# A decode attention kernel whose VectorE, ScalarE and sync-engine programs become loops with token waits

## The chip, the cores and the metric

The kernel runs on one core of a Trainium2 chip. The metric is the device time of one execution in microseconds (us), as the median of several runs. The profile is of one execution; its times count from the first instruction of the program.

## What is computed

One decode step of a transformer block, in float32, batch 1, one query token. Attention has 32 query heads in 8 groups; each group of 4 shares one key and value cache of 65536 rows by 128. The attention output and then a bilinear gated layer are added to the residual.

```python
B, Sq, D = x.shape                       # 1, 1, 512
Hq, Dh, Hkv = 32, 128, 8                 # cache: 8 x 65536 x 128, K and V
q = (layernorm(x) @ wq).reshape(...)     # 32 heads
scores = einsum("bhqd,bhkd->bhqk", q, k) * (Dh ** -0.5)
o = einsum("bhqk,bhkd->bhqd", softmax(scores), v)
h = x + o.reshape(B, Sq, Hq * Dh) @ wo
n = layernorm(h)
y = h + ((n @ w_gate) * (n @ w_up)) @ w_down   # 512 -> 1792 -> 512
```

## The kernel before

Each of the 8 cache heads is read in 4 K chunks and then 4 V chunks of 8.39 MB (128 partitions by 16384 values). Two SBUF buffers, `kv[0]` and `kv[1]`, take the chunks in turn, so a chunk can be fetched only when the one two before it has been used up. The sync engine (SP) issues all the large transfers, in one queue, in program order (lines 111 to 144): the first query weights `wq0`, the chunks, between V1 and V2 of each head one transfer `wqo` of 2.1 MB with the next head's query weights and this head's output weights, and at the end the gate, up and down weights `wg`, `wu`, `wd` into the two freed chunk buffers. The last V chunk, `wu` and `wd` are cut into pieces so that TensorE can begin on each piece as it lands.

TensorE (PE) already runs the heads as a hardware loop (line 388). A head there is: 16 small matmuls for the query (L333); for each K chunk 32 matmuls into a PSUM bank `psc` (L343); the softmax's transposes and small matmuls (L349 to L361); for each V chunk 32 matmuls into `pva` (L371); the sum over partitions (L378) and the output projection into `attn` (L384). Its waits are token waits: `take(s, n)` waits until semaphore `s` has `n` and subtracts them, so the same instruction serves every head.

The other engines have the 8 heads written out one after another, with waits on counters that only rise. ScalarE (ACT) copies each `psc` to SBUF (L210) and takes the exponentials (L235). VectorE (DVE) takes the maxima (L216), copies the transposes (L240), handles `orow`, `o_pad`, and adds the head's part to `acc` (L258). SP waits for a value of TensorE's counter, `pe.sem`, before each chunk (L116). After the loop the last head's sum goes to `arow` (L266), which also gives the sum for the second layer norm; the gate and up projections (L406), the product (L289) and the down projection (L437) follow, and the output is sent from L299.

The names in rows: `kv<-in_kT` and `kv<-in_v` are chunk transfers, `psc`, `ptp`, `pva`, `attn`, `sm` are PSUM banks. L315 is the `take` of TensorE.

Of the kernel before, what the change touches and what calls it, by code (L numbers as in the profile page):

```python
# [8 lines left out]
P = 128  # L9
# [13 lines left out]
PE_ONLY = bass.OrderedEngineSet([mybir.EngineType.PE])  # L23
# [20 lines left out]
def body(nc, xr, kT, v, wq0, wqo, wo7, wg, wu, wd, out):  # L44
# [33 lines left out]
    orow, acc, arow = tile("orow", P, 512), tile("acc", P, 512), tile("arow", P, 512)  # L78
# [14 lines left out]
    pe, dve, act, pool = (Counter(sem(n)) for n in ("pe", "dve", "act", "pool"))  # L93
    tok, atok = sem("tok"), sem("atok")
# [10 lines left out]
    def pe_at(h, m):  # L105
        return M_HEAD * h + m


# [3 lines left out]
    done = []  # L112
    for h in range(HKV):
        for i in range(2 * NT):
            if len(done) >= 2:
                sp.wait_ge(pe.sem, done[-2])  # L116
            buf = len(done) % 2
            if i == NT + 2:
                sp.wait_ge(pe.sem, pe_at(h, M_Q))
                if h < LAST:  # L120
                    sp.dma_start(wqo_sb, wqo[h]).then_inc(s_w, 16)
                else:
                    sp.dma_start(wo_sb, wo7).then_inc(s_w, 16)
            if h == LAST and i == 2 * NT - 1:
                for p, (lo, hi) in enumerate(zip(V_CUTS, V_CUTS[1:])):
                    cs = slice(lo * 512, hi * 512)
                    sp.dma_start(kv[buf][:, cs], v[h, i - NT][:, cs]).then_inc(s_vp[p], 16)
            else:
                src = kT[h, i] if i < NT else v[h, i - NT]
                whole = i == 2 * NT - 1  # L130
                sp.dma_start(kv[buf], src).then_inc(s_vp[0] if whole else s_kv[buf], 16)
                for p in s_vp[1:] if whole else ():

                    sp.sem_inc(p, 16)
            done.append(pe_at(h, M_K + i if i < NT else M_V + i - NT))
    sp.wait_ge(pe.sem, pe_at(LAST, M_V + 2))
# [4 lines left out]
    sp.wait_ge(pe.sem, pe_at(LAST, M_V + 3))  # L141
# [64 lines left out]
    for h in range(HKV):  # L206
# [5 lines left out]
        dve_e.wait_ge(pe.sem, pe_at(h, M_Q))  # L212
        dve_e.tensor_copy(q_pad[:, 28:28 + REP], sm[0][:, 0:REP]).then_inc(tok, 1)
        for s in range(NT):
            dve_e.wait_ge(act.sem, copies[s])
            i = dve_e.tensor_reduce(out=mx[:, s:s + 1], in_=sc[s], axis=AX.X, op=ALU.max)  # L216
            if s < 2:

                i.then_inc(tok, 1)
            else:  # L220
                dve.tick(i)
        dve_self()
        dve_e.tensor_reduce(out=m1, in_=mx, axis=AX.X, op=ALU.max).then_inc(tok, 1)
        dve_e.wait_ge(pe.sem, pe_at(h, M_MX))
        dve.tick(dve_e.tensor_reduce(
            out=mrow, in_=sm[1][0:1, 0:P].rearrange("p (g h) -> p h g", h=REP), axis=AX.X, op=ALU.max))
        dve_self()
        dve_e.tensor_copy(mexp, mrow.unsqueeze(1).to_broadcast([1, 32, REP])).then_inc(tok, 1)
        dve_e.wait_ge(pe.sem, pe_at(h, M_MB))
        c_bias = dve.tick(dve_e.tensor_scalar(  # L230
            out=nbias, in0=sm[0][:, 0:1], scalar1=-SCALE, scalar2=None, op0=ALU.mult))

        act_e.wait_ge(dve.sem, c_bias)
        for s in range(NT):
            act_e.activation(  # L235
                sc[s], sc[s], AF.Exp, bias=nbias[:, 0:1], scale=SCALE,
                accum_out=sums[:, s:s + 1]).then_inc(atok, 1)
        for s in range(NT):
            dve_e.wait_ge(pe.sem, pe_at(h, M_T + s))
# [21 lines left out]
    tail0 = pe_at(LAST, M_HEAD)
    (T_AC, T_G, T_PV, T_U, T_F0, T_F1, T_D) = range(tail0 + 1, tail0 + 8)

    dve_e.wait_ge(dve.sem, c_acc)
    dve_e.wait_ge(pe.sem, tail0)
    c_arow = dve.tick(dve_e.scalar_tensor_tensor(  # L266
        out=arow, in0=attn, scalar=1.0, in1=acc, op0=ALU.mult, op1=ALU.add, accum_out=rsum[:, 0:1]))
    dve_self()
    c_nmean = dve.tick(dve_e.tensor_scalar(
        out=nmean, in0=neg_mean, scalar1=rsum[:, 0:1], scalar2=None, op0=ALU.mult))  # L270
    dve_e.wait_ge(pe.sem, T_AC)
    c_hn = dve.tick(dve_e.tensor_copy(hn_pad[:, :, 0], sm[1][:, 0:KT]))
    dve_self()
    dve.tick(dve_e.tensor_tensor(out=ln_q2, in0=hn_pad[:, :, 0], in1=hn_pad[:, :, 0], op=ALU.mult))
    dve_self()
    c_s3 = dve.tick(dve_e.tensor_reduce(out=ln_s3, in_=ln_q2, axis=AX.X, op=ALU.add))
    act_e.wait_ge(pe.sem, T_PV)
    c_t3 = act.tick(act_e.activation(ln_t3, sm[0][:, 0:1], AF.Sqrt, bias=eps_t[:, 0:1], scale=1.0))
    dve_e.wait_ge(act.sem, c_t3)
    c_r3 = dve.tick(dve_e.reciprocal(ln_r3, ln_t3))  # L280

    act_e.wait_ge(dve.sem, c_r3)
    c_g = act.tick(act_e.activation(g_sb, psc[1][:, :FJ], AF.Copy, scale=ln_r3[:, 0:1]))
    dve_e.wait_ge(act.sem, c_g)
    dve_e.wait_ge(pe.sem, T_U)
    c_f = []
# [5 lines left out]
    dve_e.wait_ge(pe.sem, T_F0)
    c_fp0 = dve.tick(dve_e.tensor_copy(f_pad[:, 0:8, 0], sm[0][:, 0:8]))
    dve_e.wait_ge(pe.sem, T_F1)
    c_fp1 = dve.tick(dve_e.tensor_copy(f_pad[:, 8:NC, 0], sm[1][:, 0:6]))
    dve_e.wait_ge(pe.sem, T_D)
# [31 lines left out]
    take(s_wq, 16)  # L328

    def head():  # L330
# [4 lines left out]
        i.then_inc(pe.sem, 1)  # L335
        take(tok)
        for s in range(NT):
            take(s_kv[s % 2], 16)
            if s >= 2:
                take(tok)  # L340
# [6 lines left out]
            i.then_inc(pe.sem, 1)  # L347
        take(tok)
        pe_e.transpose(sm[1][0:1, 0:P], m1, ident).then_inc(pe.sem, 1)  # L349
        take(tok)  # L350
        mm(sm[0][:, 0:1], mexp.rearrange("p g h -> p (g h)"), ones[0:1, 0:1],  # L351
           start=True, stop=True).then_inc(pe.sem, 1)
        for s in range(NT):
            take(atok)
            if s >= 2:
                take(tok)
            for b in range(4):
                i = pe_e.transpose(ptp[s % 2][:, b * P:(b + 1) * P], sc[s][:, b * P:(b + 1) * P], ident)  # L358
            i.then_inc(pe.sem, 1)
        take(tok, 3)  # L360
        mm(sm[1][:, 0:REP], ones, l4, start=True, stop=True).then_inc(pe.sem, 1)  # L361
        for j in range(4):
            mm(pva[32 * j:32 * j + 32, :], zeros[:, 0:32], zeros, start=True, stop=False)  # L363
        for n in range(NT):
            vt = kv[n % 2]
            pieces = list(zip(V_CUTS, V_CUTS[1:])) if n == NT - 1 else [(0, 32)]
            for p, (lo, hi) in enumerate(pieces):
                take(s_vp[p] if len(pieces) > 1 else s_kv[n % 2], 16)
# [6 lines left out]
            i.then_inc(pe.sem, 1)  # L375
        take(tok)
# [9 lines left out]
        i.then_inc(pe.sem, 1)  # L386
# [4 lines left out]
    pe_e.wait_ge(dve.sem, c_arow)  # L391
    for k in range(KT):
        mm(sm[1][:, k:k + 1], arow[:, k * P:(k + 1) * P], sel_1, start=(k == 0), stop=False)
    pe_e.wait_ge(dve.sem, c_nmean)
    mm(sm[1][:, 0:KT], nmean, ones[:, 0:KT], start=False, stop=True).then_inc(pe.sem, 1)
    pe_e.wait_ge(dve.sem, c_hn)

    def project(acc, w, sems):
# [21 lines left out]
    i.then_inc(pe.sem, 1)  # L420
    pe_e.wait_ge(dve.sem, c_f[1])
# [17 lines left out]
    i.then_inc(pe.sem, 1)  # L439
# [41 lines left out]
```

## Time and profile before

| | us |
|---|---|
| median of 3 runs | 1309.79 (1309.71 to 1310.42) |
| span of the profiled execution, first to last instruction | 1308.5 |
| TensorE matmul busy | 712.9 (54% of the span) |
| VectorE busy | 73.5 (6%) |
| ScalarE busy | 47.2 (4%) |
| DMA queue of the large transfers, share of the 16 DMA engines | 99.7% |
| data read | 564.66 MB, 432 GB/s over the span |

The page gives busy time by engine, the span in 40 slices, the DMA queues and the chain of work that ended last. Behind it are views of single instructions in order of time, of waits, of one source line, and of stretches of the span. In these, "PEq" is TensorE's sequencer (its waits and branches), "SPq" the issuing of a transfer by SP. "Idle before" is the time in which the engine did nothing before a group, with what ended it. The granted TensorE clock averages 0.738 of full.

### The profile page before, as it was taken

The numbers are of one execution on the slowest core, as the hardware profiler recorded it, in microseconds if no ns is written. First come the engines' busy times: TensorE is split into PE (matmuls) and PEld (weight loads), VectorE is DVE, ScalarE is ACT, GpSimd is POOL, SyncE is SP. The second block draws the span as 40 slices with busy tenths as digits, with TensorE's granted clock in tenths as the row PEclk, the third lists the DMA queues.
The fourth block names the chain that finished last, engine by engine and source line by source line (L and its number), as shares of the span: only waits on it lengthen the run. The fifth ranks groups of instructions, "written<-read, shape, count | busy, mean of one in ns | idle before, by whom it ended". The sixth has DMA issues, their size and how long they took to land. (4 is left out here: it accounts for less than half of the span.)

```text
span 1308.5 us, 10559 instructions
## 1 busy us (share of the span) xinstructions
PE 712.9 (54%) x4938; PEld 249.0 (19%) x4938; DVE 73.5 (6%) x181; ACT 47.2 (4%) x102; POOL 2.5 (0%) x13
## 2 busy tenths in 40 slices
PE   5366384553755446563564636636365465655556
PEld 3012031210312112120131202212021121311113
DVE  0000000100001000010000100001000010000101
ACT  0000000100001000010000100001000010000100
POOL 0000000000000000000000000000000000000000
PEclk9777666776767867767767867678677677687778
DMA  9999999999999999999999999999999999999998
GB/s 417 427 435 445 421 445 425 441 425 441 425 441 425 441 429 441 441 429 437 429 439 427 441 425 441 427 441 437 435 435 431 439 417 450 425 441 425 441 420 374
DMA packets 12260, 564.80 MB, mean 432 GB/s; under 512 B 1365, under 2 KB 1369, under 8 KB 2010
## 3 DMA queue, kind: packets, MB, share of 16 engines
q1 hardware_dynamic: 12248, 564.67, 99.7%
q8 instruction: 6, 0.10, 0.0%
q14 instruction: 4, 0.03, 0.0%
q10 hardware_dynamic: 2, 0.00, 0.0%
HBM read 564.66 MB, written 0.00 MB: 432 GB/s over the span
## 5 line engine op out<-in xcount | busy, mean ns | idle before, releaser
L343 PE MATMUL psc<-kv,q_pad 128*32 128x512 f32 x2048 | 294.6, 740 | 256.2 <-PEq L315 256.2
L371 PE MATMUL pva<-kv,pt 128*16 128x512 f32 x2048 | 280.1, 707 | 276.9 <-PEq L315 276.8
L343 PEld LDWEIGHTS psc<-kv,q_pad 128*32 128x32 f32 x2048 | 81.3, 133 | 463.0 <-issue 463.0
L371 PEld LDWEIGHTS pva<-kv,pt 128*16 128x16 f32 x2048 | 67.1, 110 | 492.7 <-issue 492.7
L210 ACT COPY sc<-psc 128x512 f32<-128x512 f32 x32 | 18.7, 585 | 1144.3 <-PE psc L343 1144.3
L216 DVE TENSOR_REDUCE mx<-sc 128x1 f32<-128x512 f32 x32 | 21.9, 686 | 538.3 <-ACT sc L210 538.3
L333 PEld LDWEIGHTS sm<-xn,wqo_sb 128*128 128x128 f32 x256 | 49.1, 299 | 10.4 <-issue 10.4
L333 PE MATMUL sm<-xn,wqo_sb 128*128 128x1 f32 x256 | 49.8, 329 | 2.2 <-issue 2.2
L250 DVE COPY orow<-pva 128x512 f32<-128x512 f32 x8 | 5.5, 692 | 566.8 <-PE pva L371 566.8
L358 PE MATMUL ptp<-ident,sc 128*128 128x128 f32 x128 | 29.3, 396 | 10.2 <-PEq L315 9.7
L358 PEld LDWEIGHTS ptp<-ident,sc 128*128 128x128 f32 x128 | 21.4, 202 | 15.5 <-issue 14.7
L235 ACT ACTIVATE sc<-sc,nbias 128x512 f32<-128x512 f32 x32 | 22.7, 711 | 20.2 <-DVE nbias L230 20.2
L240 DVE COPY pt<-ptp 128x512 f32<-128x512 f32 x32 | 22.1, 691 | 21.6 <-PE ptp L358 21.6
L363 PE MATMUL pva<-zeros 128*32 128x512 f32 x64 | 12.9, 890 | 0.0
L384 PE MATMUL attn<-wqo_sb,o_pad 128*32 128x512 f32 x64 | 10.8, 749 | 3.4 <-PEq L315 3.4
L378 PE MATMUL sm<-sel_b,orow 128*128 128x4 f32 x64 | 8.2, 252 | 7.2 <-PEq L315 7.2
L378 PEld LDWEIGHTS sm<-sel_b,orow 128*128 128x128 f32 x64 | 7.7, 191 | 14.4 <-issue 14.4
L349 PE MATMUL sm<-ident,m 128*1 128x128 f32 x8 | 2.2, 269 | 13.6 <-PEq L315 13.6
L406 PE MATMUL psc<-kv,hn_pad 128*32 128x448 f32 x64 | 8.2, 651 | 1.9 <-DMA kv<-in_wu 1.0
L361 PE MATMUL sm<-l,ones 128*128 128x4 f32 x16 | 3.9, 312 | 9.6 <-PEq L315 9.6
L351 PE MATMUL sm<-ones,mexp 1*128 1x1 f32 x16 | 3.4, 279 | 5.7 <-PEq L315 5.7
L235 ACT ACTIVATION_READ_ACCUMULATOR sc<-sc,nbias 128x1 f32 x32 | 6.0, 187 | 0.0
(88 smaller groups left out, 68.6 us busy)
## 6 DMA issues: line engine op xcount, KB each, us to landing
wqo_sb<-in_wqo SPq DMA_DIRECT2D x7, 2048.0 KB, 15.2
kv<-in_v SPq DMA_DIRECT2D x1, 4096.0 KB, 21.7
kv<-in_wg SPq DMA_DIRECT2D x1, 3584.0 KB, 18.8
kv<-in_v SPq DMA_DIRECT2D x1, 2048.0 KB, 26.2
kv<-in_v SPq DMA_DIRECT2D x2, 1024.0 KB, 29.1
kv<-in_wu SPq DMA_DIRECT2D x1, 1792.0 KB, 23.0
kv<-in_wu SPq DMA_DIRECT2D x2, 896.0 KB, 25.5
kv<-in_wd SPq DMA_DIRECT2D x1, 1536.0 KB, 19.7
```

Of the source, the lines that this page charges most:

```text
L210: copies.append(act.tick(act_e.copy(sc[s], psc[s % 2])))
L216: i = dve_e.tensor_reduce(out=mx[:, s:s + 1], in_=sc[s], axis=AX.X, op=ALU.max)
L235: act_e.activation(sc[s], sc[s], AF.Exp, bias=nbias[:, 0:1], scale=SCALE, accum_out=sums[:, s:s + 1]).then_inc(atok, 1)
L240: dve_e.tensor_copy(pt[s].rearrange("p g b h -> p b g h"), ptp[s % 2].rearrange("p (b g h) -> p b g h", b=4, h=REP)).then_inc(tok, 1)
L333: i = mm(sm[0][:, r:r + 1], wq_sb[:, k, r * P:(r + 1) * P], xn[:, k:k + 1], start=(k == 0), stop=(k == KT - 1))
L343: i = mm(psc[s % 2][32 * j:32 * j + 32, :], q_pad[:, 28 - 4 * rs:60 - 4 * rs], kv[s % 2][:, (4 * rs + j) * 512:(4 * rs + j + 1) * 512], st ...
L358: i = pe_e.transpose(ptp[s % 2][:, b * P:(b + 1) * P], sc[s][:, b * P:(b + 1) * P], ident)
L363: mm(pva[32 * j:32 * j + 32, :], zeros[:, 0:32], zeros, start=True, stop=False)
L371: i = mm(pva[32 * j:32 * j + 16, :], pt[n][:, 8 * j + rs, :, :].rearrange("p b h -> p (b h)"), vt[:, w * 512:(w + 1) * 512], start=False, ...
L378: i = mm(sm[0][:, 0:REP], orow[:, b * P:(b + 1) * P], sel_b[:, 4 * b:4 * b + 4], start=(b == 0), stop=(b == 3))
L384: i = mm(attn[32 * r:32 * r + 32, :], o_pad[:, r, :], wo_sb[:, r, :], start=True, stop=True)
L406: i = mm(acc[32 * j:32 * j + 32, :FJ], hn_pad[:, k, :], w[:, o:o + FJ], start=(k == 0), stop=(k == KT - 1))
```

## The change

ScalarE, VectorE and SP get hardware loops over the heads. SP's loop has 7 rounds and the last head is written out behind it; the addresses of the chunks come from registers. TensorE's one rising counter is replaced by tokens: `pd` (TensorE to VectorE), `pa` (TensorE to ScalarE), `ad` and `da` (between ScalarE and VectorE), `own` (VectorE to itself), and `free`, one for each chunk buffer that may be filled. `free` is raised twice by SP at the start, by ScalarE for each K chunk, by TensorE for V0, V1 and V2, and by VectorE for V3. The three engines' programs begin with an alignment to a multiple of 128 instructions. The last head is no longer a special case on VectorE: every round runs the fused add with the row sum, into `acc`, and `arow` is gone.

```diff
+    def take(e, s, n=1):
+        e.wait_ge(s, n).then_inc(s, -n)
+
+    for e in (sp, act_e, dve_e):
+        e.addr_align(SLOTS, 0, max_nops=0)
...
+    sp.sem_inc(free, 2)
+
+    def chunks(h, last):
         for i in range(2 * NT):
-            if len(done) >= 2:
-                sp.wait_ge(pe.sem, done[-2])
-            buf = len(done) % 2
+            take(sp, free)
+            buf = i % 2
...
+    with nc.Fori(0, LAST, engines=SP_ONLY) as h:
+        chunks(h, False)
+    chunks(LAST, True)
...
-    for h in range(HKV):
-        copies = []
-        for s in range(NT):
-            act_e.wait_ge(pe.sem, pe_at(h, M_K + s))
-            copies.append(act.tick(act_e.copy(sc[s], psc[s % 2])))
+    with nc.Fori(0, HKV, engines=ACT_ONLY):
+        for s in range(NT):
+            take(act_e, pa)
+            act_e.sem_inc(free, 1)
+            act_e.copy(sc[s], psc[s % 2]).then_inc(ad, 1)
+        take(act_e, da)
...
+    with nc.Fori(0, HKV, engines=DVE_ONLY):
+        take(dve_e, pd)
...
-        dve_e.wait_ge(pe.sem, pe_at(h, M_V + NT - 1))
+        take(dve_e, pd)
+        dve_e.sem_inc(free, 1)
         dve_e.tensor_copy(orow, pva).then_inc(tok, 1)
...
-            c_acc = dve.tick(dve_e.tensor_tensor(out=acc, in0=attn, in1=acc, op=ALU.add))
+        take(dve_e, pd)
+        dve_e.scalar_tensor_tensor(
+            out=acc, in0=attn, scalar=1.0, in1=acc, op0=ALU.mult, op1=ALU.add,
+            accum_out=rsum[:, 0:1]).then_inc(own, 1)
+        take(dve_e, own)
...
-            i.then_inc(pe.sem, 1)
+            i.then_inc(pd if n == NT - 1 else free, 1)
```

On SP, one head before, from its third chunk on; `[waits pe]` is the wait on TensorE's counter, part of the transfer's own row:

```order
L131 DMA kv0<-in_kT 128x16384 [waits pe]
L131 DMA kv1<-in_kT 128x16384 [waits pe]
L131 DMA kv0<-in_v 128x16384 [waits pe]
L131 DMA kv1<-in_v 128x16384 [waits pe]
L121 DMA wqo_sb<-in_wqo 128x4096 [waits pe]
L131 DMA kv0<-in_v 128x16384
L131 DMA kv1<-in_v 128x16384 [waits pe]
```

The same engine in the changed kernel, from the start of its program; an ISA row at L128 or L125 is register arithmetic on an address, ahead of which the token is taken:

```order
L110 ISA [waits barrier_Pool_Activation_PE_DVE_SP_release]
L114 DMA wqo_sb<-in_wq0 128x2048
L138 UNCONDITIONAL_BRANCH
L128 ISA [waits free]
L128 DMA kv0<-in_kT 128x16384
L128 DMA kv0<-in_v 128x16384 [waits free]
L128 DMA kv1<-in_v 128x16384 [waits free]
L125 ISA [waits free]
L125 DMA wqo_sb<-in_wqo 128x4096
L134 DMA kv1<-in_v 128x16384 [waits free]
L138 REGISTER_ALU
L138 COMPARE_AND_BRANCH
```

The order of the transfers is the same; ahead of the first one stands the alignment (L110), and between it and the first chunk the loop's entry, a token and the address arithmetic.

On ScalarE before, the first head and the end of the program (ACT_TABLE_LOAD loads a function table; it stands once for the exponentials and once for the second square root, without a wait):

```order
L210 COPY sc<-psc 128x512 [waits pe] x4
L235 ACT_TABLE_LOAD
L235 ACTIVATE sc,sums<-sc,nbias 128x512 [waits dve]
L235 ACTIVATE sc,sums<-sc,nbias 128x512 x3
L278 ACT_TABLE_LOAD
L278 ACTIVATE ln_t<-sm,eps_t 128x1 [waits pe]
L283 ACTIVATE g_sb<-psc,ln_r 128x448 [waits dve]
```

On ScalarE in the changed kernel, the loop and what follows it:

```order
L215 ACT_TABLE_LOAD [waits pa]
L215 COPY sc<-psc 128x512
L215 COPY sc<-psc 128x512 [waits pa] x3
L218 ACTIVATE sc,sums<-sc,nbias 128x512 [waits da]
L218 ACTIVATE sc,sums<-sc,nbias 128x512 x3
L211 REGISTER_ALU
L211 COMPARE_AND_BRANCH
L277 ACT_TABLE_LOAD [waits pa]
L277 ACTIVATE ln_t<-sm,eps_t 128x1
L283 ACTIVATE g_sb<-psc,ln_r 128x448 [waits da]
```

The table load has moved into the loop, ahead of the copy of K0 and behind its token, and the load for the second square root now stands behind TensorE's token as well. In the loop's code the `sem_inc(free, 1)` stands between the token and the table load.

## Rows read from the trace of the kernel before

**Rows 1.** The page: the 40 slices, mean busy share of the DMA engines, in tenths.

```profile
DMA  9999999999999999999999999999999999999998
```

**Rows 2.** The page, DMA queues: packets, MB, share of 16 engines.

```profile
q1 hardware_dynamic: 12248, 564.67, 99.7%
q8 instruction: 6, 0.10, 0.0%
q14 instruction: 4, 0.03, 0.0%
```

**Rows 3.** Stretches of the span: us, busy by engine, granted clock, DMA share, GB/s.

```profile
core 0: us, PE busy (x) PEld busy (x) DVE busy (x) ACT busy (x) POOL busy (x), PEclk, DMA share, GB/s
0.00:2.00 2.00, 0.00 (x0) 0.00 (x0) 0.31 (x3) 0.72 (x1) 1.25 (x9) 1.00 0.29 34
2.00:100.00 98.00, 48.88 (x308) 21.53 (x309) 6.48 (x24) 6.45 (x12) 1.23 (x6) 0.81 1.01 437
...
1100.00:1200.00 100.00, 55.99 (x368) 19.99 (x368) 3.76 (x7) 1.75 (x3) 0.00 (x0) 0.72 1.00 433
...
1306.00:1308.50 2.50, 0.37 (x8) 0.10 (x8) 0.29 (x1) 0.00 (x0) 0.00 (x0) 1.00 0.00 1
```

**Rows 4.** Line L131, the chunk transfers from 30 us on.

```profile
L131 SPq DMA_DIRECT2D kv<-in_v x31: 327/328/447, 74.7 to 1227.1; - x31
L131 SPq DMA_DIRECT2D kv<-in_kT x30: 327/328/328, 34.1 to 1170.7; - x30
...
DMA to landing us min/median/max: 26.9/29.4/35.9
```

**Rows 5.** The chain that ended last, its end: start us, us, what.

```profile
1283.06 22.84 DMA kv<-in_wd
1305.90 0.04 issue
1305.94 0.47 PE pva L437 x8
1306.41 0.02 issue
1306.44 0.29 DVE y L297
```

**Rows 6.** In order of time, the start: start us, us, what [idle before].

```profile
0.73 0.52 ACTq L109 DMA_DIRECT2D x_row<-in_xr  x1
...
0.73 0.40 SPq L111 DMA_DIRECT2D wqo_sb<-in_wq  x1
...
1.20 0.88 SPq L131 DMA_DIRECT2D kv<-in_kT  x2
...
2.27 0.34 PE L320 MATMUL psc<-ones,x_row 1*128 1x1 f32 x1 [2.27 <-DMA x_row<-in_xr]
```

**Rows 7.** The page, DMA issues: KB each, us to landing.

```profile
wqo_sb<-in_wq SPq DMA_DIRECT2D x1, 1024.0 KB, 4.8
```

**Rows 8.** Line L388, the branches of TensorE's loop, ns.

```profile
L388 PEldq COMPARE_BRANCH  x8: 88/223/238, 179.0 to 1283.7; - x8
```

**Rows 9.** In order of time: a VectorE result taken by token, and a chunk's end.

```profile
103.69 0.23 DVE L245 TENSOR_SCALAR l<-sel_h,l 128x4 f32<-128x4 f32 x1
104.03 0.50 PEld L361 LDWEIGHTS sm<-l,ones 128*128 128x128 f32 x2 [1.57 <-issue]
...
197.47 0.33 SPq L131 DMA_DIRECT2D kv<-in_kT  x1
197.48 0.58 ACT L210 COPY sc<-psc 128x512 f32<-128x512 f32 x1 [96.55 <-PE psc L343]
```

**Rows 10.** VectorE's and ScalarE's waits: us in total, times, longest.

```profile
ACT sc L210 <- PE psc L343: 1144.3, 32, 96.5
...
DVE q_pad L213 <- PE sm L333: 43.9, 8, 7.1
```

**Rows 11.** Lines L235 and L278: table loads, ns and start.

```profile
L235 ACT ACT_TABLE_LOAD  x1: 1283/1283/1283, 95.2 to 95.2; - x1
L278 ACT ACT_TABLE_LOAD  x1: 1283/1283/1283, 1215.1 to 1215.1; - x1
```

**Rows 12.** In order of time, the end of the program.

```profile
1288.68 4.78 PE L406 MATMUL psc<-kv,hn_pad 128*32 128x448 f32 x32 [0.87 <-DMA kv<-in_wg]
...
1294.29 0.64 ACT L283 ACTIVATE g_sb<-psc,ln_r 128x448 f32<-128x448 f32 x1 [0.23 <-DVE ln_r L280]
...
1297.39 0.96 PE L406 MATMUL psc<-kv,hn_pad 128*32 128x448 f32 x8 [1.02 <-DMA kv<-in_wu]
1298.51 0.81 DVE L289 SCALAR_TENSOR_TENSOR f_sb<-psc,ln_r,g_sb 128x256 f32<-128x256 f32 x2 [4.25 <-PE psc L406]
...
1303.47 2.28 PE L437 MATMUL pva<-kv,f_pad 128*32 128x128 f32 x56 [0.84 <-DMA kv<-in_wd]
```

More of the change, by code (lines that the diff above doesn't have):

```diff
@@ L22 @@
 LAST = HKV - 1
-PE_ONLY = bass.OrderedEngineSet([mybir.EngineType.PE])
+PE_ONLY, DVE_ONLY, ACT_ONLY, SP_ONLY = (bass.OrderedEngineSet([e]) for e in (
+    mybir.EngineType.PE, mybir.EngineType.DVE, mybir.EngineType.Activation, mybir.EngineType.SP))
+SLOTS = 128
 V_CUTS = (0, 16, 24, 28, 32)
@@ L77, in body @@
     l4, linv = tile("l4", P, REP), tile("linv", P, REP)
-    orow, acc, arow = tile("orow", P, 512), tile("acc", P, 512), tile("arow", P, 512)
+    orow, acc = tile("orow", P, 512), tile("acc", P, 512)
     rsum, nmean = tile("rsum", P, 1), tile("nmean", P, P)
@@ L91, in sem @@
         return sems[-1]
-    pe, dve, act, pool = (Counter(sem(n)) for n in ("pe", "dve", "act", "pool"))
-    tok, atok = sem("tok"), sem("atok")
+    dve, act, pool = (Counter(sem(n)) for n in ("dve", "act", "pool"))
+    tok, atok, pd, pa, ad, da, own, free = (
+        sem(n) for n in ("tok", "atok", "pd", "pa", "ad", "da", "own", "free"))
     s_kv = [sem("s_kv0"), sem("s_kv1")]
@@ L103, in body @@
     wd_t = kv[1]
-    def pe_at(h, m):
-        return M_HEAD * h + m
+    def take(e, s, n=1):
+        e.wait_ge(s, n).then_inc(s, -n)
+    for e in (sp, act_e, dve_e):
+        e.addr_align(SLOTS, 0, max_nops=0)
     act_e.dma_start(x_row, xr).then_inc(s_xr, 16)
     sp.dma_start(wq_sb, wq0).then_inc(s_wq, 16)
-    done = []
-    for h in range(HKV):
+    sp.sem_inc(free, 2)
+    def chunks(h, last):
         for i in range(2 * NT):
-            if len(done) >= 2:
-                sp.wait_ge(pe.sem, done[-2])
-            buf = len(done) % 2
+            take(sp, free)
+            buf = i % 2
             if i == NT + 2:
-                sp.wait_ge(pe.sem, pe_at(h, M_Q))
-                if h < LAST:
+                if last:
+                    sp.dma_start(wo_sb, wo7).then_inc(s_w, 16)
+                else:
                     sp.dma_start(wqo_sb, wqo[h]).then_inc(s_w, 16)
-                else:
-                    sp.dma_start(wo_sb, wo7).then_inc(s_w, 16)
-            if h == LAST and i == 2 * NT - 1:
+            src = kT[h, i] if i < NT else v[h, i - NT]
+            if i < 2 * NT - 1:
+                sp.dma_start(kv[buf], src).then_inc(s_kv[buf], 16)
+            elif last:
                 for p, (lo, hi) in enumerate(zip(V_CUTS, V_CUTS[1:])):
                     cs = slice(lo * 512, hi * 512)
-                    sp.dma_start(kv[buf][:, cs], v[h, i - NT][:, cs]).then_inc(s_vp[p], 16)
+                    sp.dma_start(kv[buf][:, cs], src[:, cs]).then_inc(s_vp[p], 16)
             else:
[L129 to L132, printed above, removed]
+                sp.dma_start(kv[buf], src).then_inc(s_vp[0], 16)
+                for p in s_vp[1:]:
                     sp.sem_inc(p, 16)
-            done.append(pe_at(h, M_K + i if i < NT else M_V + i - NT))
-    sp.wait_ge(pe.sem, pe_at(LAST, M_V + 2))
+    with nc.Fori(0, LAST, engines=SP_ONLY) as h:
+        chunks(h, False)
+    chunks(LAST, True)
+    take(sp, free)
     sp.dma_start(wg_t, wg).then_inc(s_wg, 16)
@@ L140, in body @@
         sp.dma_start(wu_t[:, cs], wu[:, cs]).then_inc(s_wu[p], 16)
-    sp.wait_ge(pe.sem, pe_at(LAST, M_V + 3))
+    take(sp, free)
     for p, (lo, hi) in enumerate(zip(D_CUTS, D_CUTS[1:])):
@@ L237, in body @@
                 accum_out=sums[:, s:s + 1]).then_inc(atok, 1)
+    with nc.Fori(0, HKV, engines=DVE_ONLY):
+        take(dve_e, pd)
+        dve_e.tensor_copy(q_pad[:, 28:28 + REP], sm[0][:, 0:REP]).then_inc(tok, 1)
         for s in range(NT):
-            dve_e.wait_ge(pe.sem, pe_at(h, M_T + s))
+            take(dve_e, ad)
+            dve_e.tensor_reduce(out=mx[:, s:s + 1], in_=sc[s], axis=AX.X, op=ALU.max).then_inc(
+                tok if s < 2 else own, 1)
+        take(dve_e, own, 2)
+        dve_e.tensor_reduce(out=m1, in_=mx, axis=AX.X, op=ALU.max).then_inc(tok, 1)
+        take(dve_e, pd)
+        dve_e.tensor_reduce(
+            out=mrow, in_=sm[1][0:1, 0:P].rearrange("p (g h) -> p h g", h=REP), axis=AX.X,
+            op=ALU.max).then_inc(own, 1)
+        take(dve_e, own)
+        dve_e.tensor_copy(mexp, mrow.unsqueeze(1).to_broadcast([1, 32, REP])).then_inc(tok, 1)
+        take(dve_e, pd)
+        dve_e.tensor_scalar(
+            out=nbias, in0=sm[0][:, 0:1], scalar1=-SCALE, scalar2=None, op0=ALU.mult).then_inc(da, 1)
+        for s in range(NT):
+            take(dve_e, pd)
             dve_e.tensor_copy(
@@ L242, in body @@
                 ptp[s % 2].rearrange("p (b g h) -> p b g h", b=4, h=REP)).then_inc(tok, 1)
-        dve.tick(dve_e.tensor_reduce(out=l1, in_=sums, axis=AX.X, op=ALU.add))
-        dve_self()
+        dve_e.tensor_reduce(out=l1, in_=sums, axis=AX.X, op=ALU.add).then_inc(own, 1)
+        take(dve_e, own)
         dve_e.tensor_scalar(
             out=l4, in0=sel_h, scalar1=l1[:, 0:1], scalar2=None, op0=ALU.mult).then_inc(tok, 1)
-        dve_e.wait_ge(pe.sem, pe_at(h, M_L))
-        dve.tick(dve_e.reciprocal(linv, sm[1][:, 0:REP]))
@@ L249, in body @@
-        dve_e.wait_ge(pe.sem, pe_at(h, M_V + NT - 1))
+        take(dve_e, pd)
+        dve_e.reciprocal(linv, sm[1][:, 0:REP]).then_inc(own, 1)
+        take(dve_e, pd)
+        dve_e.sem_inc(free, 1)
         dve_e.tensor_copy(orow, pva).then_inc(tok, 1)
-        dve_self()
-        dve_e.wait_ge(pe.sem, pe_at(h, M_PO))
+        take(dve_e, own)
+        take(dve_e, pd)
         dve_e.tensor_tensor(
             out=o_pad[:, :, 0], in0=sm[0][:, 0:REP], in1=linv, op=ALU.mult).then_inc(tok, 1)
-        if h < LAST:
-            dve_e.wait_ge(dve.sem, c_acc)
-            dve_e.wait_ge(pe.sem, pe_at(h, M_AT))
-            c_acc = dve.tick(dve_e.tensor_tensor(out=acc, in0=attn, in1=acc, op=ALU.add))
@@ L261, in body @@
[L261 to L286, printed above, removed]
+        take(dve_e, pd)
+        dve_e.scalar_tensor_tensor(
+            out=acc, in0=attn, scalar=1.0, in1=acc, op0=ALU.mult, op1=ALU.add,
+            accum_out=rsum[:, 0:1]).then_inc(own, 1)
+        take(dve_e, own)
+    dve_e.sem_inc(tok, 1)
+    dve_e.tensor_scalar(
+        out=nmean, in0=neg_mean, scalar1=rsum[:, 0:1], scalar2=None, op0=ALU.mult).then_inc(tok, 1)
@@ new lines, in body @@
+    take(dve_e, pd)
+    dve_e.tensor_copy(hn_pad[:, :, 0], sm[1][:, 0:KT]).then_inc(own, 1)
+    take(dve_e, own)
+    dve_e.sem_inc(tok, 1)
+    dve_e.tensor_tensor(
+        out=ln_q2, in0=hn_pad[:, :, 0], in1=hn_pad[:, :, 0], op=ALU.mult).then_inc(own, 1)
+    take(dve_e, own)
+    dve_e.tensor_reduce(out=ln_s3, in_=ln_q2, axis=AX.X, op=ALU.add).then_inc(tok, 1)
+    take(act_e, pa)
+    act_e.activation(
+        ln_t3, sm[0][:, 0:1], AF.Sqrt, bias=eps_t[:, 0:1], scale=1.0).then_inc(ad, 1)
@@ L287, in body @@
+    take(dve_e, ad)
+    dve_e.reciprocal(ln_r3, ln_t3).then_inc(da, 1)
+    take(act_e, da)
+    act_e.activation(g_sb, psc[1][:, :FJ], AF.Copy, scale=ln_r3[:, 0:1]).then_inc(ad, 1)
+    take(dve_e, ad)
+    take(dve_e, pd)
     for half in range(2):
         cs = slice(half * 256, min(FJ, half * 256 + 256))
-        c_f.append(dve.tick(dve_e.scalar_tensor_tensor(
+        dve_e.scalar_tensor_tensor(
             out=f_sb[:, cs], in0=psc[0][:, cs], scalar=ln_r3[:, 0:1], in1=g_sb[:, cs],
-            op0=ALU.mult, op1=ALU.mult)))
@@ L292, in body @@
[L292 to L296, printed above, removed]
+            op0=ALU.mult, op1=ALU.mult).then_inc(tok, 1)
+    take(dve_e, pd)
+    dve_e.tensor_copy(f_pad[:, 0:8, 0], sm[0][:, 0:8]).then_inc(tok, 1)
+    take(dve_e, pd)
+    dve_e.tensor_copy(f_pad[:, 8:NC, 0], sm[1][:, 0:6]).then_inc(tok, 1)
+    take(dve_e, pd)
@@ L327, in body @@
     pe_e.wait_ge(dve.sem, c_const)
-    take(s_wq, 16)
+    take(pe_e, s_wq, 16)
     def head():
@@ L334, in head @@
                        start=(k == 0), stop=(k == KT - 1))
-        i.then_inc(pe.sem, 1)
-        take(tok)
+        i.then_inc(pd, 1)
+        take(pe_e, tok)
         for s in range(NT):
-            take(s_kv[s % 2], 16)
+            take(pe_e, s_kv[s % 2], 16)
             if s >= 2:
-                take(tok)
+                take(pe_e, tok)
             for rs in range(8):
@@ L367, in head @@
             for p, (lo, hi) in enumerate(pieces):
-                take(s_vp[p] if len(pieces) > 1 else s_kv[n % 2], 16)
+                take(pe_e, s_vp[p] if len(pieces) > 1 else s_kv[n % 2], 16)
                 for w in range(lo, hi):
@@ L374, in head @@
                            start=False, stop=(n == NT - 1 and rs == 7))
-            i.then_inc(pe.sem, 1)
-        take(tok)
+            i.then_inc(pd if n == NT - 1 else free, 1)
+        take(pe_e, tok)
         for b in range(4):
@@ L379, in head @@
                    start=(b == 0), stop=(b == 3))
-        i.then_inc(pe.sem, 1)
-        take(s_w, 16)
-        take(tok)
+        i.then_inc(pd, 1)
+        take(pe_e, s_w, 16)
+        take(pe_e, tok)
         for r in range(REP):
@@ L385, in head @@
                    start=True, stop=True)
-        i.then_inc(pe.sem, 1)
+        i.then_inc(pd, 1)
     with nc.Fori(0, HKV, engines=PE_ONLY, hint_back_edge=True):
         head()
-    pe_e.wait_ge(dve.sem, c_arow)
+    take(pe_e, tok)
     for k in range(KT):
[L393 to L396, printed above, removed]
+        mm(sm[1][:, k:k + 1], acc[:, k * P:(k + 1) * P], sel_1, start=(k == 0), stop=False)
+    take(pe_e, tok)
+    mm(sm[1][:, 0:KT], nmean, ones[:, 0:KT], start=False, stop=True).then_inc(pd, 1)
+    take(pe_e, tok)
     def project(acc, w, sems):
@@ L407, in project @@
                        start=(k == 0), stop=(k == KT - 1))
-        i.then_inc(pe.sem, 1)
+        return i
     project(psc[1], wg_t, [s_wg])
-    pe_e.wait_ge(dve.sem, c_s3)
-    mm(sm[0][:, 0:1], mean_m, ln_s3, start=True, stop=True).then_inc(pe.sem, 1)
+    take(pe_e, tok)
+    mm(sm[0][:, 0:1], mean_m, ln_s3, start=True, stop=True).then_inc(pa, 1)
     for j in range(4):
-        mm(pva[32 * j:32 * j + 32, 0:P], sel_pad, arow[:, j * P:(j + 1) * P], start=True, stop=False)
-    project(psc[0], wu_t, s_wu)
-    pe_e.wait_ge(dve.sem, c_f[0])
+        mm(pva[32 * j:32 * j + 32, 0:P], sel_pad, acc[:, j * P:(j + 1) * P], start=True, stop=False)
+    project(psc[0], wu_t, s_wu).then_inc(pd, 1)
+    take(pe_e, tok)
     for b in range(2):
@@ L419, in body @@
                start=(b == 0), stop=(b == 1))
-    i.then_inc(pe.sem, 1)
-    pe_e.wait_ge(dve.sem, c_f[1])
+    i.then_inc(pd, 1)
+    take(pe_e, tok)
     mm(sm[1][:, 0:4], f_sb[:, 2 * P:3 * P], sel_q, start=True, stop=False)
@@ L426, in body @@
                 start=False, stop=True)
-    i2.then_inc(pe.sem, 1)
+    i2.then_inc(pd, 1)
     fill(4)
-    pe_e.wait_ge(dve.sem, c_fp0)
+    take(pe_e, tok)
     for c in range(NC):
         if c == 8:
-            pe_e.wait_ge(dve.sem, c_fp1)
+            take(pe_e, tok)
         if c in D_CUTS:
```

45 lines of the change are left out of this document (11 added, 34 removed).

## Prediction

> **What bounds the kernel now.** I read the page first: in its slices the reader sees the DMA engines at nine tenths or more in 39 of 40 slices [rows 1], and in its queues one queue with 99.7% of the 16 engines' time [rows 2]. TensorE is at 54%, VectorE at 6%, ScalarE at 4%. An average could still hide gaps at the head boundaries, so the second view is the span cut into stretches [rows 3]: from 2 us on the DMA share is 1.00 (a share a little above 1 is packets counted where they start), at 433 to 437 GB/s, whatever TensorE and its clock do in the stretch; it falls to 0.00 only behind 1306 us. The stream of 564.67 MB therefore sets the time, and the kernel is three pieces: about 1.8 us before data flows (up to 2.00 us the share is 0.29), the stream up to the last landing at 1305.90, and 2.6 us of closing work to 1308.5.
>
> The third view says how much delay this stream can bear. SP issues a chunk when the one two before it is used up, and from then a chunk takes 26.9 us at least and 29.4 in the median until it lands, over 61 chunks [rows 4]. Alone, 8.39 MB at 433 GB/s take 19.4 us. So at each issue the queue still held 26.9 - 19.4 = 7.5 us of earlier work at the least, 10 us in the median. I call this the lead: a delay of the issue below 7.5 us moves no byte.
>
> The fourth view is the end of the chain [rows 5]: the last piece of `wd` lands at 1305.90, eight matmul records (0.47 us), VectorE's copy (0.29 us) and the output's transfer follow. Between them lie 0.04 and 0.02 us.
>
> **The change part by part.** The sum is made against the profiled execution, 1308.5 us of span; the median of the runs is 1309.79, which is 1.29 us more around the span. I leave these 1.29 us as they are.
>
> *SP's start.* Ahead of the first transfer, at 0.73 us [rows 6], stands the alignment. If the padding is jumped over, that is one branch. The only branches in the trace are those that close TensorE's loop: 88 ns the one that fell through, 223 to 238 ns those that were taken [rows 8], so 0.09 to 0.24 us where the code is already there; I take 0.15, near the middle, since the jump goes forward and compares nothing. Nothing hides this: all bytes come later by it. Between `wq` and the first chunk come a semaphore write, the loop's entry, a token and the arithmetic on the address. A token is priced by a row: VectorE's `l4` ends at 103.92 and TensorE, which takes a token for it, starts loading at 104.03 [rows 9], so 0.11 us, against 0.04 for a wait in the instruction itself [rows 5]; with a branch and two register steps like it this makes 0.5 to 0.8 us. `wq` lands 4.8 us after its issue [rows 7], at 5.5 us, and the chunk's issue moves from 1.20 to at most 2.0; from the issue of a small transfer to the matmul that uses it lie 2.27 - 0.73 = 1.54 us [rows 6], so its first bytes would be there by 3.6. Hidden, with 1.9 us in hand.
>
> *SP's chunk waits.* Each of the 64 chunks is now released by a token. For K chunks ScalarE stands between: TensorE, ScalarE's token, its `free`, SP's token. Before, SP and ScalarE reacted to the same end of a chunk within 0.01 us, at 197.47 and 197.48 [rows 9], so the added hop is two tokens, 0.22 us, and at the most 0.5 with the address arithmetic. ScalarE is never late for it: it waited 1144.3 us in total at these copies [rows 10], and `free` is raised before the copy and the table load. V3 goes over VectorE, which likewise waits there. Against a lead of 7.5 us: 0. With the lead gone it would cost 64 x 0.2 to 0.5 = 13 to 32 us, and that is what this term would be in a kernel with single chunks in flight.
>
> *Back edges.* SP's comes behind V3's issue, when its next token is more than ten microseconds away. ScalarE's comes after the exponentials, a whole V phase before its next token. VectorE's is the tight one: it comes behind the add to `acc`, and next is `q_pad`, for which VectorE waited 43.9 us in 8 heads, 5.5 each [rows 10]. With a branch of 0.24 and a token of 0.11 it keeps 5 us.
>
> *Table loads.* ScalarE's load of 1.28 us [rows 11] is now done in every head, ahead of the copy of K0. VectorE and TensorE get that copy 1.28 us later, and TensorE needs its `psc` bank again only for K2, two chunk landings of 19.4 us later: 0. At the end the load stood at 1215.1, out of the way; now it stands behind TensorE's token at about 1293.8, so `g_sb` moves from 1294.29 + 0.64 = 1294.93 to about 1296.3. The product that needs it began at 1298.51, behind `wu`'s last piece and the matmuls of 1297.39 [rows 12]. It has 2.2 us left: 0.
>
> *The last head's end.* VectorE's fused add is now followed by a token to itself, the loop's closing branch (88 ns when it falls through [rows 8]) and another semaphore write before TensorE goes on: 0.3 to 0.5 us. TensorE later waits 0.87 us for `wg`, 1.02 for `wu` and 0.84 for `wd` [rows 12], so each such delay is taken up by the next landing. Behind the product two PSUM copies with tokens add some 4 x 0.07 = 0.3 us, against the 0.84. Behind the last landing only VectorE's wait ahead of `y` becomes a token: 0.11 - 0.04 = 0.07 us, on the path.
>
> *Less code to load.* The instruction queues move 0.13 MB of 564.80 [rows 2]. At 432 GB/s the four packets of q14, 0.03 MB, are 0.07 us of the stream; they lie inside the span before and should go.
>
> Sum: 0.15 + 0.07 - 0.07 = +0.15 us. 1309.79 + 0.15 is 1309.9.
>
> **The rivals.** About 0.2%, 2.6 us, is what a measurement of this kernel can tell from no change.
>
> *A: the start waits for code (slower).* The alignment puts SP's first transfer into another block of code than the barrier ahead of it. If that block isn't there, SP stands still between the barrier and `wq`, and the whole stream with it, since there is no lead yet. The trace shows no such fetch, so the nearest rows bound it: a small transfer from issue to use, 1.54 us [rows 6], to the 4.8 us of `wq` under the first load [rows 7]. That gives 1311.4 to 1314.7; it is slower in my sense from a stall of 2.5 us on. Against it speaks that before, SP went from barrier to transfer without a pause the trace shows, and that ahead of the span there is time for loading. Taken at 3 us: 1312.9.
>
> *B: back edges that wait for code (slower, much).* The same fetch at each of VectorE's or SP's branches, in the full stream. VectorE has 5 us, then 7.5 us of lead: below 12.5 us nothing is seen, which a fetch of 1.5 to 4.8 us doesn't reach. If it had to wait like a chunk, 29.4 us, each of 7 heads would lose up to 17 us: 1309.8 + 119 = 1429. In its favour is only that the trace of before shows just TensorE's back edges, at 0.24 us. The Trainium skill speaks for this rival: "Runtime: NRT & Kernel Launch", section "Instruction fetch mechanics", says that a taken branch to code outside the blocks held must wait for a fetch, and so prefers unrolled code. In this trace TensorE's loop pays no such wait, and the loops of the change are far shorter than TensorE's; by that rule, too, they would stay inside what is held.
>
> *C: faster.* Only what lies outside the stream can shrink: 1.8 + 2.6 + 1.3 = 5.7 us. To gain 2.6 the shorter programs would have to halve it; I see no row for that. Nor would loops that did not save any fetch show: that is the forecast plus 0.07.
>
> **How the numbers follow.** Forecast 0.87: 1309.9, with 1309.0 to 1311.0 from the terms' own bounds (0.09 to 0.24 at the start, 0 to 0.2 at the end, and the runs' own spread of 0.7). A 0.09, half of it below the line of 1312.4 and half above. B 0.02. C 0.02. So faster 0.02, same 0.91, slower 0.07. The range takes the forecast's and the lower part of A: 1308.9 to 1311.8.
>
> **What would show it.** In the changed kernel's profile: the DMA share still 1.00 in every stretch; SP's first transfer within 0.3 us of the barrier (if it stands 1.5 us or more behind it, A); chunks that land 26 us or more after their issue, some 0.3 us less than before; eight table loads at the K0 copies and ScalarE still waiting there; q14 without packets in the span; the last `wd` landing 2.6 us before the end. Wrong would be a stretch with a share under 0.99 in mid-span, or a chain whose end is no longer `wd`.

## The result, and the profile after

The changed kernel takes 1312.37 us in the median of 18 runs (1311.99 to 1315.87), the kernel before 1309.86 in 18 runs (1309.71 to 1310.42); the ratio is 1.0021, 95% interval 1.0014 to 1.0028. It is 2.5 us slower. The forecast was 1309.9, at most 1311.8. The profiled execution spans 1311.4 us, against 1308.5; with 1312.75 us it is 0.4 us above the median of the runs.

The stream is as full as before. The page of the changed kernel, its DMA slices and queues (as [rows 1, 2]):

```profile
DMA  9999999999999999999999999999999999999998
...
q1 hardware_dynamic: 12248, 564.67, 99.5%
q8 instruction: 6, 0.10, 0.0%
q14 instruction: 3, 0.02, 0.0%
```

The stretches of the changed kernel (columns as in [rows 3]) show where it is not: in the first 4 us no data flow, only the three packets of q14 (12 GB/s up to 2 us).

```profile
0.00:2.00 2.00, 0.00 (x0) 0.00 (x0) 0.32 (x3) 0.00 (x0) 1.23 (x9) 1.00 0.04 12
2.00:4.00 2.00, 0.00 (x0) 0.00 (x0) 0.00 (x0) 0.22 (x1) 1.24 (x6) 1.00 0.00 0
4.00:100.00 96.00, 45.87 (x301) 19.63 (x301) 6.33 (x23) 4.95 (x7) 0.00 (x0) 0.83 1.01 436
```

In order of time, the start of the changed kernel (start us, us, what), to be read beside [rows 6]:

```profile
1.19 2.56 ACTq L112 DMA_DIRECT2D x_row<-in_xr  x1
1.23 2.33 SPq L114 DMA_DIRECT2D wqo_sb<-in_wq  x1
1.41 0.17 DVE L169 MEMSET ones<- 128x128 f32 x1 [1.41 <-PEq L469]
...
4.06 0.36 SPq L128 DMA_DIRECT2D kv<-in_kT  x1
```

SP's first transfer starts 0.5 us later, at 1.23 instead of 0.73, and its issue takes 2.33 us instead of 0.40. ScalarE's first transfer shows the same, 2.56 against 0.52. VectorE, aligned like them, only starts later (1.41 against 0.83) and then runs at once. SP's issue ends at 3.56 instead of 1.13: 2.43 us, which is the loss but for a rest. The packets of q14, of the kind "instruction", carry code, 0.01 MB each; I call them code packets. All three of the span are here; from 2.5 us to the end there is none. The DMA queues between 1.5 and 2.5 us:

```profile
q14 instruction: 3, 0.02, 8.5%
```

At the other end, the last landing and the copy behind it (as [rows 5]):

```profile
1308.73 0.43 PE L433 MATMUL pva<-kv,f_pad 128*32 128x128 f32 x8 [0.19 <-DMA kv<-in_wd]
1309.33 0.29 DVE L296 COPY y<-pva 128x128 f32<-128x128 f32 x1 [5.53 <-DVEq L107]
```

The last piece's matmuls come 2.79 us later than before (1305.94), the copy 2.89 (1306.44). So of 2.9 us in this execution 2.43 are lost at the start, 0.1 behind the last landing, and 0.36 are added inside the stream. The median loss of 2.5 us is as large as the first two together.

### The profile page after: what moved, and what is told of

It is laid out like the page before. It is cut to its first block, busy times and chain, and to the rows that moved or that the text cites. A ratio compares the mean times of both kernels' runs of the same rounds, so it can differ in the third digit from the quotient of the medians.

```text
span 1311.4 us, 11033 instructions
## 1 busy us (share of the span) xinstructions
PE 705.4 (54%) x4938; PEld 250.2 (19%) x4938; DVE 73.4 (6%) x188; ACT 56.1 (4%) x109; POOL 2.5 (0%) x13
## 5 line engine op out<-in xcount | busy, mean ns | idle before, releaser
L367 PE MATMUL pva<-kv,pt 128*16 128x512 f32 x2048 | 275.0, 697 | 276.4 <-PEq L107 276.4
L359 PE MATMUL pva<-zeros 128*32 128x512 f32 x64 | 8.5, 605 | 0.0
```

The source lines that it names most:

```text
L367: i = mm(pva[32 * j:32 * j + 16, :], pt[n][:, 8 * j + rs, :, :].rearrange("p b h -> p (b h)"), vt[:, w * 512:(w + 1) * 512], start=False, ...
```

## The experiments

**Theories.** *Alignment*: SP's first transfer is held because of the alignment. *Loops* (rival): loop entry, tokens and register addresses delay the transfers. *Any fetch* (rival): the code fetches, whichever engine they are for, delay the first data.

A *block* is here a stretch of 128 instructions, the unit of the alignment, and a *slot* a place in it; a block is *fresh* when the engine comes to it for the first time by a jump. A *fetch* shows as a code packet. The *hold* is the time by which the issue of a transfer is longer than its 0.40 us (SP) or 0.52 us (ScalarE) before.

### Which part of the change, and which engine

`e1_no_align`: the change without its alignments.

```diff
-    for e in (sp, act_e, dve_e):
-        e.addr_align(SLOTS, 0, max_nops=0)
```

> The loops and tokens of the change, without the alignment on any engine. If the alignment makes the loss: 1309.8 to 1310.2, the issue of wq 0.4 us long at 0.73 as before, first data near 1.8 us. If the loops make it (SP's loop entry, tokens, addresses from registers): still 1312.4, with wq or the first chunk late. If a loop now lies across two blocks of code, the code queue q14 has 7 or more packets in the span, and by the forecast's lead of 7.5 us the time doesn't show them.

`e2_align_not_sp` aligns ScalarE and VectorE, `e3_align_sp_only` only SP.

```diff
-    for e in (sp, act_e, dve_e):
+    for e in (act_e, dve_e):      # e2
+    for e in (sp,):               # e3
```

> The change with the alignment left out on SP alone. If the loss is SP's own issue that stands while code is fetched for SP: 1309.8 to 1310.2, wq issued in 0.4 us, x_row on ScalarE still some 2.5 us long. If the code fetches of any engine hold up the first data in the DMA engines: 1311.4 to 1312.4.

> The change with the alignment on SP alone. SP's own issue stands: 1312.2 to 1312.6, wq's issue 2.3 us long, x_row's 0.5. Fetches of any engine: one fetch instead of three, 1310.5 to 1311.5.

`e4_before_aligned`: the kernel before, heads written out, with the three alignments.

```diff
+    for e in (sp, act_e, dve_e):
+        e.addr_align(128, 0, max_nops=0)
     act_e.dma_start(x_row, xr).then_inc(s_xr, 16)
```

> The kernel before, written out head by head, with the three alignments ahead of its first transfers. If the alignment makes the loss, with no part for the loops: 1312.2 to 1312.6, wq's issue 2.3 us long. If the loops make it: 1309.9.

| kernel | median us | ratio to before, 95% | span of the profiled execution | its time less its span | SP's first issue |
|---|---|---|---|---|---|
| before | 1309.86 | | 1308.5 | 1.3 | 0.73, 0.40 long |
| changed | 1312.37 | 1.0014 to 1.0028 | 1311.4 | 1.35 | 1.23, 2.33 long |
| e1 | 1310.57 | 0.9999 to 1.0019 | 1308.5 | 1.9 | 0.74, 0.40 long |
| e2 | 1310.64 | 0.9999 to 1.0018 | 1308.5 | 1.9 | 0.74, 0.40 long |
| e3 | 1312.32 | 1.0012 to 1.0031 | 1311.5 | 1.4 | 1.23, 2.11 long |
| e4 | 1313.24 | 1.0017 to 1.0037 | 1310.7 | 2.4 | 1.20, 2.45 long |

The start of e3 (SP aligned):

```profile
0.74 0.51 ACTq L112 DMA_DIRECT2D x_row<-in_xr  x1
...
1.23 2.11 SPq L114 DMA_DIRECT2D wqo_sb<-in_wq  x1
```

and of e2 (ScalarE and VectorE aligned):

```profile
0.74 0.40 SPq L114 DMA_DIRECT2D wqo_sb<-in_wq  x1
1.19 2.29 ACTq L112 DMA_DIRECT2D x_row<-in_xr  x1
```

The hold follows the alignment of each engine, and costs time only on SP. Loops falls: without SP's alignment the loops' span is that of the kernel before, 1308.5 (e1, e2), and with it the written-out heads have the loss too (e4). Any fetch falls: in e2 two code packets run between 1.5 and 4 us, and wq is not late.

The times of e1, e2 and e4 lie above what was expected, by 0.4 to 0.6 us: they are 0.6 to 1.1 us longer than their spans explain. In each a code packet runs behind the span. The DMA queues of e1 from 1308.5 us on:

```profile
q14 instruction: 1, 0.01, 0.3%
```

Such a packet is there in e1, e2, e4, e9 and e12, and in the later e10, e13 and e14 (1.9 to 2.4 us around the span); it is missing before, after and in e3, e5, e6, e7, e8 and e11 (1.3 to 1.4). A code packet behind the span thus goes with 0.6 to 1.1 us more around it; that is a correlation over sixteen kernels, no experiment of its own, and that it depends on where in its block a program ends is a guess.

### What holds the transfer

`e11_same_block`: SP jumps as before, but to slot 60, inside the block it is in.

```diff
-        e.addr_align(SLOTS, 0, max_nops=0)
+        e.addr_align(SLOTS, 60, max_nops=0)     # SP alone
```

> SP alone is aligned, to slot 60: a jump ahead of wq as before, but, if SP's program starts near slot 50, inside the block that it is in. If the jump itself makes the hold: wq's issue 2 us long, span 1311. If entering a fresh block and its fetch make it: no q14 packet near 1.8 us, wq's issue 0.4 us long at 1.23, span 1308.9 to 1309.1.

Measured: 1310.26 (0.9996 to 1.0016), span 1309.2.

```profile
0.74 0.51 ACTq L112 DMA_DIRECT2D x_row<-in_xr  x1
0.90 0.40 SPq L114 DMA_DIRECT2D wqo_sb<-in_wq  x1
```

No code packet runs here between 1 and 180 us, where e3 has one between 1.7 and 1.8. The jump alone costs 0.16 us and holds nothing; into the fresh block it cost 0.49 (1.23 in e3 against 0.74). The span is 0.1 us above the expected range.

`e7_sixteen_steps` and `e12_forty_steps`: SP alone aligned, then semaphore writes of no use, then wq.

```diff
+    spare = sem("spare")
+    for _ in range(16):           # e12: 40
+        sp.sem_inc(spare, 1)
     sp.dma_start(wq_sb, wq0).then_inc(s_wq, 16)
```

> The alignment on SP alone, and behind it 16 extra semaphore writes on SP ahead of wq (about 0.06 us each, 1.0 us). If SP's transfers are held until the fetch is over, the writes run inside the hold: wq starts at 2.2 and ends near 3.4 as before, time 1312.2 to 1312.5. If the first transfer behind an alignment has a cost of its own of 2.1 us: 1.0 later, 1313.2 to 1313.5.

> SP alone aligned, with 40 extra semaphore writes ahead of wq (2.5 us). If the hold ends at a fixed time (3.4 to 3.6 us), wq starts near 3.7 and its issue takes 0.4 us: span 1311.3 to 1311.7. If a first transfer in a fresh block is slow by itself (1.3 us or more): wq done at 5.0 or later, span 1312.3 and up.

Measured: e7 1312.42 (1.0011 to 1.0030), the same as without the writes. SP's issues in e7:

```profile
2.23 1.33 SPq L117 DMA_DIRECT2D wqo_sb<-in_wq  x1
4.04 0.95 SPq L131 DMA_DIRECT2D kv<-in_kT  x2
```

and in e12 (span 1311.4, time 1313.84 with a code packet behind the span):

```profile
3.62 0.40 SPq L117 DMA_DIRECT2D wqo_sb<-in_wq  x1
4.50 0.96 SPq L131 DMA_DIRECT2D kv<-in_kT  x2
```

The writes run at once, 40 of them in 2.4 us (1.23 to 3.62): SP does not lack its own code. Only the transfer is held, and until about 3.5 us however late it is asked for (3.56 in e7, 3.34 in e3); asked for at 3.62, it takes 0.40. The end follows the code packet: it starts between 1.7 and 1.8 us in e3 and between 1.8 and 1.9 in e7, and the issue ends 1.5 to 1.8 us later.

`e5_wq_first` aligns SP behind the issue of wq, `e6_head0_first` behind the whole of head 0, which is written out. Neither aligns the other engines.

```diff
     sp.dma_start(wq_sb, wq0).then_inc(s_wq, 16)
+    sp.addr_align(SLOTS, 0, max_nops=0)          # e5
...
+    chunks(0, False)                             # e6
+    sp.addr_align(SLOTS, 0, max_nops=0)
+    with nc.Fori(1, LAST, engines=SP_ONLY) as h:
```

> The loops and tokens, aligned on SP alone and only behind the issue of wq. If entering a fresh block starts a code fetch that holds SP's next transfer for some 2.1 us: wq issued at 0.73 in 0.4 us, the first chunk's issue long (about 2.2 us, ending near 4), so that only the part beyond wq's 3.9 us of cover is lost, 0.3 to 1.0 us: span 1308.8 to 1309.6, time 1310.2 to 1311.0. If the loss came with whatever SP does first: wq long again, 1312.3.

> Head 0 written out on SP ahead of the alignment, the loop for heads 1 to 6 behind it; nothing aligned on ScalarE and VectorE. If the fetch holds SP only where it enters the block, it now falls into SP's wait at the head's end: wq at 0.73, first chunk by 1.5, span 1308.4 to 1308.6, and with no code fetched behind the last transfer 1309.7 to 1310.0, the same as the kernel before. If the aligned loop itself costs time: over 1311.

e5: 1311.21 (1.0000 to 1.0019; 1310.21 to 1312.72), span 1310.2. Its first two chunks:

```profile
2.16 0.96 SPq L126 DMA_DIRECT2D kv<-in_kT  x2
```

They were not held, though the code packet ran only at 5.1 us, behind wq's data. So "held while a fetch is open", as I had it, falls too: a long first chunk was expected. The span is all the same 1.7 us above before and above the expected 1308.8 to 1309.6. In mid-stream its chunks land some 0.65 us later than before, and the last piece of `wd` is used 1.57 us later (1307.51 against 1305.94), so the rest is lost behind the last chunk. No hold explains that, and the cause stays open. e6: 1310.19 (0.9997 to 1.0015), span 1308.9; the time is 0.2 and the span 0.3 us above the expected range, which I can't account for.

`e8_align_mid`: SP aligned in the last head, between a token and K2's issue.

```diff
             take(sp, free)
+            if last and i == 2:
+                sp.addr_align(SLOTS, 0, max_nops=0)
```

> Nothing aligned at the start; SP alone is aligned in the last head, between the token for K2 and K2's issue. If the hold belongs to the fetch and not to the start of a program: that one issue row is 2 us long or more (longer than at the start, if the fetch has to wait behind chunks), against 0.33 before, and the lead of 7.5 us takes it: span 1308.4 to 1308.7. If it belongs to the start: 0.33.

Measured: 1309.86 (0.9990 to 1.0010 of before), span 1308.5. The issue behind the alignment, and the DMA queues from 1157 to 1157.5 us:

```profile
1152.81 0.33 SPq L127 DMA_DIRECT2D kv<-in_kT  x1
```

```profile
q14 instruction: 1, 0.01, 3.9%
```

Not held, with a fetch open. Either the hold belongs to the start of a program, or to an engine's first transfer. Three kernels separate these, `e10_first_mid`, `e13_second_mid` and `e14_first_mid_plain`: in e10 and e14 x_row goes over SP, so that ScalarE has issued nothing yet, in e13 over ScalarE; in all three ScalarE issues the last head's `wo` behind its loop.

```diff
+    act_e.addr_align(SLOTS, 0, max_nops=0)       # e10, e13; not e14
+    act_e.dma_start(wo_sb, wo7).then_inc(s_w, 16)
```

> No alignment at the start; x_row goes over SP behind wq, and ScalarE, aligned behind its loop, issues the last head's wo, its first transfer of the program, in mid-stream. If a first transfer of an engine is held by the fetch of a fresh block: ScalarE's issue row is 2 us long or more. If the hold belongs to the start of the program alone: 0.5 us, as x_row took before. The span moves by less than 0.3 us either way.

> As the kernel in which ScalarE, aligned behind its loop, issues the last head's wo in mid-stream (there its first transfer, 6.82 us long), but ScalarE has issued x_row at the start, so that this is its second. If only an engine's first transfer waits for the fetch of a fresh block: about 0.5 us. If ScalarE's transfers always wait for it, or any transfer that directly follows the jump: 5 to 8 us.

> The same wo from ScalarE in mid-stream as its first transfer, without the alignment. If the hold needs the fresh block: about 0.5 us. If a first transfer in a full stream is slow by itself: 5 to 8 us, and then the alignment is not what held it.

ScalarE's issue in e10, its first transfer, behind the alignment:

```profile
1215.14 6.82 ACTq L218 DMA_DIRECT2D wqo_sb<-in_wo  x1
```

in e13, its second, behind the alignment:

```profile
1215.99 0.37 ACTq L218 DMA_DIRECT2D wqo_sb<-in_wo  x1
```

in e14, its first, not aligned:

```profile
1215.41 0.37 ACTq L217 DMA_DIRECT2D wqo_sb<-in_wo  x1
```

Both conditions are needed: the engine's first transfer of the program, and the fetch that entering a fresh block sets off. In e10 the code packet starts between 1220.4 and 1220.5 us, behind queued chunks, and the issue ends at 1221.96, again 1.5 us later. In e13 the packet runs in the same microsecond, and the transfer has long gone. In e14 no code packet runs from 1210 us to 1308. Each of the three was executed once, e13 and e14 on another chip than e10. The spans of these three single runs, 1309.8, 1309.6 and 1310.0, are 1.1 to 1.5 us above before, not under 0.3 as e10's expectation had it; all three share the moved `wo`, and I leave open what makes their spans longer.

### A loop across two blocks

`e9_dve_across` aligns VectorE alone, to slot 80, so that a block ends inside its loop.

```diff
-    for e in (sp, act_e, dve_e):
-        e.addr_align(SLOTS, 0, max_nops=0)
+    dve_e.addr_align(SLOTS, 80, max_nops=0)
```

> The loops, with only VectorE aligned, and to slot 80 of a block, so that its loop of 42 instructions should lie across a block's end; SP and ScalarE not aligned. If such a loop fetches code again at each back edge: q14 has some 14 to 17 packets in the span instead of 1. The forecast's cover (5 us at q_pad, then the lead of 7.5 us) says the span stays at 1308.4 to 1308.7 all the same; if a fetch behind queued chunks takes 25 us or more, as rival B has it, 1400 and up.

Measured: 1310.67 (0.9997 to 1.0016), span 1308.9, 1.96 us around it. The DMA queues of e9 from 100 to 112 us, and from 112 to 1308 us:

```profile
q14 instruction: 1, 0.01, 0.2%
```

```profile
q1 hardware_dynamic: 11300, 516.69, 99.8%
q8 instruction: 3, 0.05, 0.0%
```

In e1 the span's one code packet runs between 186 and 187 us, behind the end of VectorE's head 0, and where VectorE is aligned to a block's start (changed, e2) there is none in the stream. Here it runs at 109 us, in the middle of VectorE's head 0, so the block's end lies inside the loop. Then no code was fetched for seven more rounds. This loop, over two neighbouring blocks, had both at hand; its alignment could save one code packet. The span is 0.2 us above the expected range.

## Why the prediction was wrong, point by point

*The bound* was read rightly: the stream fills the DMA engines, and what moves its start moves the end. *Leads*: predicted 26 us or more from issue to landing, some 0.3 less than before; line L128 from 32 us on gives, against 26.9 and 29.4 in [rows 4]:

```profile
DMA to landing us min/median/max: 26.3/29.0/34.8
```

So tokens, hops, register addresses and SP's back edges cost nothing, as said; e1, e2 and e8 confirm it with spans of 1308.5. *Table loads*: eight in the loop, on the page's row of their group, and nothing from them:

```profile
L215 ACT ACT_TABLE_LOAD x8 | 10.3, 1283 | 695.1 <-ACTq L107 695.1
```

*The last head's end* cost more than its 0.3 to 0.5 us: from `orow` to the gate projection lie 8.22 us (1284.25 to 1292.47) instead of 7.41 (1281.27 to 1288.68), in part because the output projection's matmuls ran slower there (1.71 us against 1.06). The 0.87 us of wait for `wg` were used up, and the projection now waits for a token:

```profile
1292.47 5.49 PE L402 MATMUL psc<-kv,hn_pad 128*32 128x448 f32 x32 [0.61 <-PEq L107]
```

The later waits for data took it up, as the term had it: the last piece's matmuls stand 2.79 us later, no more than the landings.

*The tail*: 0.07 predicted behind the last landing, 0.1 measured. *Less code*: q14 was to vanish from the span. The packets of before, in the stream, are gone; three new ones stand at the start, set off by the alignments themselves.

*The step that failed is SP's start.* It put 0.15 us for a jump and nothing for the issue behind it, and the jump is that (0.16 in e11). But "where the code is already there" was the condition, and the jump goes to a fresh block: 0.49 us, and then a hold of SP's first transfer, together 2.43 us. Rival A had the place, a price that holds the measured one, 1.54 to 4.8 from [rows 6, 7], and the time, 1311.4 to 1314.7. I gave it 0.09. That its price fits is in part luck, since its bounds are the times of data transfers. The reason against it, that there is time for loading ahead of the span, was an argument without a row: the trace of before has no jump on SP, so it could not show what one sets off. The row that should have made me careful is the issue of wq itself at 0.73, which has no lead at all. Rival A's mechanism was also off: its sign was SP's first transfer 1.5 us or more behind the barrier, and the transfer came 0.5 us later than before and then took 2.33; SP had its code (e7, e12), the fetch is one that the entry into the block sets off, and only a first transfer waits for it.

*Rival B* did not come: the changed kernel has no packet of q14 from 2.5 us on, and e9, whose loop crosses a block's end, fetches once. The rule of the Trainium skill cited there ("Runtime: NRT & Kernel Launch", "Instruction fetch mechanics"), by which a jump to code that isn't held must wait for a fetch, would not have given the loss: the held instruction is a transfer whose code was there. *Rival C* did not come; the best of these kernels, e8, is level with before.

*Not settled*: 0.36 us inside the stream of the profiled execution; its landings slip once, in head 0, and then keep the delay. The size of this slip varies from kernel to kernel, and it was not tried by itself. e5's 1.7 us and the spans of e10, e13 and e14 are as open. Why an engine's first transfer waits for the fetch, the runs don't say.

## What to carry to other kernels

Where one stream of transfers fills the time, a delay behind the first few issues is free up to the lead, and a delay of the first one is paid in full: look at what a change puts ahead of the first transfer. An alignment that enters a fresh block of code belongs behind the engine's first transfer, and not right behind it: late in the stream it cost nothing (e8), behind head 0 the median was 0.3 us above before, within the noise (e6), right behind wq it was 1.3 us above, for a reason not found (e5). Loops with token waits on the other engines are a way to shorten programs at no cost in time here, and no gain either.

## What the hardware showed

An engine's first transfer of the program, asked for while the fetch set off by entering a fresh block was under way, was held: its issue took 2.1 to 2.6 us at the start (e3, after), 6.8 us in a full stream (e10), and ended 1.5 to 1.8 us behind the start of the code packet (e3, e7, e10). A second transfer (e5, e8, e13), a first one without the fetch (e11, e14), semaphore writes (e7, e12) and VectorE's operations (after) were not held. Kernels with a code packet behind their span took 0.6 to 1.1 us more around it; what makes it so was not tried.
